# Strided queries, masked copies, ranks and a drain rearranged in an attention and mixture-of-experts kernel

## The chip, the cores and the metric

The kernel runs on one core of one Trainium2 chip. The metric is the time of one execution in device microseconds. The engines are called PE (matrix products), PEld (the loading of PE's weights), DVE (VectorE), ACT (ScalarE), POOL (GpSimd) and SP (SyncE, which here issues most of the plain loads).

## The reference

Eight batches with eight heads, 576 positions and 64 values a head. Heads 0 to 3 see a local window of 32 positions; heads 4 to 7 see every 32nd earlier position ("strided"). The 4608 rows of 512 values that come out go through a layer of eight experts, of which each row uses one:

```python
mask_local = (rel >= 0) & (rel < stride)
mask_strided = (rel >= 0) & (pos[None, :] % stride == pos[:, None] % stride)
attn = softmax(where(mask, q @ k.T / 8, -1e9)) @ v          # per head
x = attn.transpose(0, 2, 1, 3).reshape(B * S, H * D)        # 4608 x 512
logits = x @ w_gate + modality_bias[modality_id]            # 8 experts
e_idx = argmax(logits);  gate_w = softmax(logits)[e_idx]
out = gate_w * (relu(x @ w1[e_idx]) @ w2[e_idx])            # 512 -> 1024 -> 512
```

## The kernel before

**Attention** (the first 190 us or so). The batches are taken as four pairs (`bp` 0 to 3). Work comes in 32 units, alternately a `Local` (one local head of a batch pair) and a `Strided` (two strided heads of one batch). Iteration n of the main loop loads unit n+3, does the scores of unit n, the transposes (`turn`) of unit n-2 and the values of unit n-3, and prepares (`prep`) unit n+2. PE runs in exactly the order in which this code is written; the other engines are ordered by a scheduler, except where `pin` keeps instructions in the order of the code. Each engine takes its own instructions in its own order, and a tile's readers wait for its writers by semaphores.

`Local.prep` writes queries into a zeroed block tile `qd`, one half on DVE, one on ACT. `Strided.prep` makes the like tile `qz` from the loaded `qks`: POOL multiplies the queries, broadcast over two halves, by a 0/1 mask (L379; for unit 0 DVE does it). `Strided.scores` multiplies `qz` by the keys into `ss`, and DVE and ACT make the normalised exponentials `ens`. `Strided.turn` transposes these into `ts` in PSUM and copies them four times, each time with another 0/1 mask per partition, into `eb`: copies 0 and 2 on DVE (L424), 1 and 3 on ACT (L422). `Strided.values` multiplies `eb` by the values `vs` into `ot`.

**Routing** of a batch pair is a generator, `finish_pair` with `route` in it, of which the main loop takes POPS = 5 steps an iteration (the expert stage two steps an f-step). It transposes the rows, forms the logits `lg` and `lt`, and marks the chosen expert of each row in `oh` (`ohb` in bf16). The rank of a row within its expert needs a running count: DVE makes `cum` by nine dependent additions (L536) after a comparison, a reduction and an addition (L531 to L534). After RK = 14 further steps two matrix products give the ranks `rk` (L540, L541), DVE makes of them the list `posi`, and POOL scatters the pair's token rows from the tile `xt` to the DRAM buffer `xd`, by nine indirect DMAs (L557). `xt` has two buffers, so the first write of pair bp+2 to its `xt` (L352, in `Local.values`) waits for the scatter of pair bp. The row numbers `tok_sb`, loaded by SP, are copied into `xt` (L527).

**Experts.** 18 slots of 256 rows each of one expert (`ffn`), then one of 128 rows (`half_ffn`). A slot has eight f-steps of matrix products h (L832) and o (L846). POOL gathers the rows (`fx`, L701) and the weights (`raw`, L717) by indirect DMAs and sends the results out (L854; L776 for the half slot). ACT and DVE split the weights into two parts, `wh` and `wl`. Slots of pairs 1 and 2 are planned before the last pair is routed (`PHASES`).

Of the kernel before, what the change touches and what calls it, by code (L numbers as in the profile page):

```python
# [11 lines left out]
F32 = mybir.dt.float32  # L12
F32R = mybir.dt.float32r
BF16 = mybir.dt.bfloat16
# [6 lines left out]
P = 128  # L21
# [6 lines left out]
E = 8  # L28
# [10 lines left out]
LT, RK = 7, 14  # L39
# [10 lines left out]
C_HALF = C_P + 1  # L50
C_T = C_HALF + 2
# [22 lines left out]
def _constants():  # L74
    cf = np.zeros((P, C_N), np.float32)
    cf[:, C_ID:C_ID + P] = np.eye(P)
    cf[:, C_RE8:C_RE8 + E] = E - np.arange(E)
    cf[:, C_H:C_H + 2] = np.arange(P)[:, None] + P * np.arange(2)
    cf[:, C_SIO:C_SIO + 32] = np.arange(32)
    cf[:, C_P] = np.arange(P)  # L80
    cf[:, C_F:C_F + 4] = P * np.arange(4)
    cf[:64, C_HALF] = 1
    cf[64:, C_HALF + 1] = 1
# [90 lines left out]
def attention_moe(ctx: ExitStack, tc: tile.TileContext, a, out):  # L174
# [13 lines left out]
    warm = pa("warm")  # L188

# [71 lines left out]
    ets = zeros(2, [P, 4, 4, 2, 32], "et")  # L261
    for t in qds + ets:
        nc.vector.memset(t[:], 0.0)

# [92 lines left out]
    class Strided:  # L357
# [17 lines left out]
        def prep(self):  # L375
            self.qz = qz = lp.tile([P, 32, 2, 18], F32, tag="qz", name=f"qz{self.n}")
            q = self.qk[:, 0, :].rearrange("p (r q) -> p r q", q=18).unsqueeze(2).to_broadcast([P, 32, 2, 18])
            half = cf[:, C_HALF:C_HALF + 2].unsqueeze(1).unsqueeze(3).to_broadcast([P, 32, 2, 18])
            (nc.gpsimd if self.n else nc.vector).tensor_tensor(qz[:], q, half, ALU.mult)  # L379
# [31 lines left out]
        def turn(self):  # L411
# [4 lines left out]
            self.eb = eb = lp.tile([72, 4, 2, 2, 72], F32, tag="eb", name=f"eb{n}")  # L416
            src = tp[0:72].rearrange("p g (j x) -> p g j x", j=2)[:, :, :, 0:36].rearrange("p g j (h q) -> p g j h q", h=2)
            for t in range(4):
                dst = eb[:, :, :, :, 18 * t:18 * t + 18]
                on = cf[0:72, C_T + t:C_T + t + 1]  # L420
                if t % 2:
                    nc.scalar.activation(dst, src, AF.Copy, scale=on)  # L422
                else:
                    nc.vector.tensor_scalar(dst, src, on, None, ALU.mult)  # L424

        def values(self):
            n, eb, vs, b = self.n, self.eb, self.vs, self.b
            for g2 in range(2):
                ot = pa(f"ot{n}{g2}")[:, :288]
                for g in (2 * g2, 2 * g2 + 1):  # L430
                    for j in range(2):
                        c = (g % 2) * 144 + 72 * j
                        for h in range(2):
# [3 lines left out]
                                eb[:, g, j, h, :],  # L437
# [36 lines left out]
    def route(bp, xt, xcs):  # L474
# [45 lines left out]
        ohb = ap.tile([P, 9, E], BF16, tag="ohb", name=f"ohb{bp}")  # L520
        nc.vector.tensor_copy(ohb[:], oh[:])
# [8 lines left out]
        cum = ap.tile([P, 10, E], BF16, tag="cum", name=f"cum{bp}")  # L530
# [3 lines left out]
        nc.vector.tensor_scalar(cum[:, 0, :], low[:], float(T2 * bp // P), None, ALU.add)  # L534
        for i in range(9):
            nc.vector.tensor_tensor(cum[:, i + 1, :], cum[:, i, :], ohb[:, i, :], ALU.add)  # L536
# [3 lines left out]
        nc.tensor.matmul(rk, cb[:, M_TRI:M_TRI + P], ohb.rearrange("p t e -> p (t e)"), start=True, stop=False)  # L540
        nc.tensor.matmul(rk, cb[:, M_ONE:M_ONE + P], cum[:, 0:9, :].rearrange("p t e -> p (t e)"), start=False, stop=True)  # L541
        po = ap.tile([P, 9, E], F32, tag="po", name=f"po{bp}")
        nc.vector.tensor_tensor(po[:], rk.rearrange("p (t e) -> p t e", t=9), oh[:], ALU.mult)
# [4 lines left out]
        new = cum[:, 0, :]  # L548
        nc.vector.tensor_tensor(fst[:, bp, :], new, cnt[:, bp, :], ALU.subtract)
        if bp:  # L550
            nc.vector.tensor_tensor(stp[:, bp, :], fst[:, bp, :], fst[:, bp - 1, :], ALU.subtract)
        else:
            nc.vector.tensor_copy(stp[:, 0, :], new)
        nc.vector.tensor_tensor(cnt[:, bp + 1, :], cum[:, 9, :], fst[:, bp, :], ALU.subtract)
# [192 lines left out]
    def half_ffn(fp, le, xs):  # L747
# [10 lines left out]
        for f in range(8):  # L758
# [13 lines left out]
            settle(LAG)  # L772
        settle(0)
# [253 lines left out]
```

## Time and profile before

| what | us |
|---|---|
| median of the runs (3) | 624.02 |
| lowest and highest | 623.73, 792.28 |
| the profiled execution: time | 620.45 |
| the profiled execution: span of its trace | 618.6 |

The profiled execution's time is 1.85 us more than its span, and the median is 3.57 us more than the profiled execution. Times in the trace count from the span's start. In the timeline a row gives the start, the duration, the engine, the line, the operation and its tiles; the brackets give how long the engine had been idle ahead of it and what ended the wait. PEclk is the clock that PE was granted, as a share of full speed.

### The profile page before, as it was taken

How to read it: one execution, taken by the hardware profiler on the slowest of the kernel's cores; microseconds unless marked ns; L12 is line 12 of the kernel's file. 1: busy time of each engine (PE TensorE's matmuls, PEld its weight loads, DVE VectorE, ACT ScalarE, POOL GpSimd, SP SyncE). 2: the span in 40 equal slices, each digit the busy share in tenths (PEclk: the TensorE clock that was granted, in tenths of full speed). 3: DMA queues.
4: the chain of work that ended last, by engine and by line, in shares of the span. 5: the costliest groups of instructions: out<-in, count | busy, mean ns of one | idle time of the engine just before them, and what ended most of it. 6: DMA issues, size and time to landing. Idle time of an engine off the chain costs nothing.

```text
span 618.6 us, 15169 instructions
## 1 busy us (share of the span) xinstructions
PE 582.8 (94%) x5979; PEld 507.3 (82%) x5979; DVE 459.2 (74%) x1141; ACT 370.7 (60%) x755; POOL 254.9 (41%) x212
## 2 busy tenths in 40 slices
PE   7989898898989999899999999999999999999991
PEld 4767785686778988798998999998989999999990
DVE  7786886895979799697687777777777777777540
ACT  2657674675657666466665666665666665666540
POOL 1242154266173558854524444533533542432210
PEclk9999999797999999999999999999999999999996
DMA  8986787699365865674744854413422457342610
GB/s 291 296 268 193 210 274 281 181 310 369 107 233 100 251 208 158 166 268 104 204 173 103 205 184 77 104 33 74 103 52 54 105 155 220 85 67 72 231 42 20
DMA packets 66158, 102.50 MB, mean 166 GB/s; under 512 B 46815, under 2 KB 48095, under 8 KB 62496
## 3 DMA queue, kind: packets, MB, share of 16 engines
q0 software_dynamic: 19744, 58.57, 28.2%
q1 hardware_dynamic: 46048, 42.47, 27.5%
q8 instruction: 49, 0.80, 0.5%
q10 hardware_dynamic: 288, 0.41, 0.2%
q14 instruction: 29, 0.24, 0.1%
HBM read 123.66 MB, written 19.43 MB: 231 GB/s over the span
## 4 chain that ended last, share of the span: by engine, by line
PE 67%; DVE 12%; DMA 10%; ACT 3%; issue 3%; POOL 2%; ACTq 0%; POOLq 0%; DVEq 0%
PE h L832 31%; PE o L846 30%; DMA xd<-xt,posi 5%; DMA raw<-in_w,wi 2%; DMA vv<-in_vl 1%; DMA tok_sb<-in_tok 1%; DVE xt L352 1%; DMA cf_sb<-in_cf 1%; DVE ex L310 1%; ACT wh L867 1%; DVE mx L309 1%; DVE eb L424 1%; POOL xd L557 1%; PE o L334 1%; DVE wl L868 1%
## 5 line engine op out<-in xcount | busy, mean ns | idle before, releaser
L868 DVE TENSOR_TENSOR wl<-raw,wh 128x512 fp32r<-128x512 f32 x288 | 186.7, 687 | 78.2 <-ACT wh L867 77.8
L867 ACT CAST wh<-raw 128x512 fp32r<-128x512 f32 x288 | 164.0, 619 | 98.2 <-PE o L846 86.2
L832 PE MATMUL h<-xh,wh 128*128 128x256 f32 x576 | 163.4, 284 | 2.1 <-ACT wh L867 1.4
L832 PE MATMUL h<-xh,wl 128*128 128x256 f32 x576 | 163.1, 284 | 0.0
L832 PE MATMUL h<-xl,wh 128*128 128x256 f32 x576 | 162.0, 282 | 0.0
L717 POOL DMA_INDIRECT raw<-in_w,wi x72 | 84.9, 1179 | 174.4 <-DVE wl L868 159.7
L832 PEld LDWEIGHTS h<-xh,wh 128*128 128x128 f32 x576 | 108.7, 189 | 9.4 <-ACT wh L867 1.8
L846 PE MATMUL o<-wh,hh 128*128 128x512 f32 x288 | 114.7, 398 | 0.3 <-ACT hh L835 0.3
L832 PEld LDWEIGHTS h<-xl,wh 128*128 128x128 f32 x576 | 108.8, 189 | 6.3
L846 PE MATMUL o<-wl,hh 128*128 128x512 f32 x288 | 113.7, 395 | 0.0
L846 PE MATMUL o<-wh,hl 128*128 128x512 f32 x288 | 112.8, 394 | 0.0
L832 PEld LDWEIGHTS h<-xh,wl 128*128 128x128 f32 x576 | 108.3, 188 | 0.8
L835 ACT ACTIVATE hh<-h 128x256 fp32r<-128x256 f32 x144 | 55.3, 385 | 47.5 <-PE h L832 47.1
L837 DVE SCALAR_TENSOR_TENSOR hl<-h,hh 128x256 fp32r<-128x256 f32 x144 | 60.5, 420 | 11.7 <-ACT hh L835 11.6
L846 PEld LDWEIGHTS o<-wh,hl 128*128 128x128 f32 x288 | 53.8, 188 | 11.9
L379 POOL TENSOR_TENSOR qz<-qks,cf_sb 128x1152 f32<-128x1152 f32 x15 | 31.7, 2113 | 74.6 <-DMA qks<-in_qks 47.7
L846 PEld LDWEIGHTS o<-wh,hh 128*128 128x128 f32 x288 | 54.3, 188 | 7.9 <-ACT hh L835 0.5
L846 PEld LDWEIGHTS o<-wl,hh 128*128 128x128 f32 x288 | 54.3, 189 | 5.8
L701 POOL DMA_INDIRECT fx<-xd,li x36 | 47.2, 1312 | 21.3 <-issue 9.1
L854 POOL DMA_INDIRECT out<-y,le x36 | 44.3, 1229 | 21.7 <-ACT y L853 14.7
L557 POOL DMA_INDIRECT xd<-xt,posi x36 | 37.3, 1036 | 29.2 <-ACT xc L442 12.7
L311 ACT ACTIVATE ex<-ex 128x256 f32<-128x256 f32 (+1 forms) x32 | 14.0, 443 | 29.4 <-DVE ex L310 29.1
(181 smaller groups left out, 771.6 us busy)
## 6 DMA issues: line engine op xcount, KB each, us to landing
qk<-in_qkl SPq DMA_DIRECT2D x16, 592.0 KB
qks<-in_qks SPq DMA_DIRECT2D x16, 576.0 KB
vv<-in_vl SPq DMA_DIRECT2D x16, 520.0 KB
vs<-in_vs SPq DMA_DIRECT2D x16, 288.0 KB
raw<-in_w,wi POOLq DMA_INDIRECT x72, 3.4
vv<-in_vl SPq DMA_DIRECT2D x16, 65.0 KB
xd<-xt,posi POOLq DMA_INDIRECT x36, 5.9
fx<-xd,li POOLq DMA_INDIRECT x36, 5.5
```

What stands on the lines that cost most here:

```text
L311: nc.scalar.activation(ex[:, g0:g0 + gn, :], ex[:, g0:g0 + gn, :], AF.Exp, scale=0.125)
L379: (nc.gpsimd if self.n else nc.vector).tensor_tensor(qz[:], q, half, ALU.mult)
L557: lists.add(nc.gpsimd.indirect_dma_start(xd[0:(bp + 1) * T2, :], IOA(ap=posi[:, i:i + 1], axis=0), xt[:, i, :], None))
L701: nc.gpsimd.indirect_dma_start(xt[:, h, :], None, xd[0:xrows, :], IOA(ap=li[:, s, h:h + 1], axis=0))
L717: ins = nc.gpsimd.indirect_dma_start(raws[j].rearrange("p f c -> p (f c)"), None, a["w"], IOA(ap=wi[:, s, j:j + 1], axis=0), bounds_check= ...
L832: nc.tensor.matmul(hp, w[:, a1], x[:, c, :], start=(k == 0), stop=(k == 11))
L835: nc.scalar.activation(hh[:], hp, AF.Relu)
L837: nc.vector.scalar_tensor_tensor(hl[:], hp, 0.0, hh.bitcast(F32), ALU.max, ALU.subtract)
L846: nc.tensor.matmul(os[h], hx[:, m], w[:, 512:1024], start=(f == 0 and i == 0), stop=(f == 7 and i == 2))
L854: outs.add(nc.gpsimd.indirect_dma_start(out, IOA(ap=le[:, h, 0:1], axis=0), y[:], None, bounds_check=NT - 1, oob_is_err=False))
L867: nc.scalar.copy(wh[:, c], raw[:, c])
L868: nc.vector.tensor_tensor(wl[:, c], raw[:, c], wh[:, c].bitcast(F32), ALU.subtract)
```

## The change

There are five parts. (1) `qz` becomes two fixed tiles, zeroed once by POOL at the start, and each strided unit's queries are written by two half copies, one on DVE and one on ACT, pinned; POOL does none of it. (2) Of the four masked copies to `eb`, the two of DVE become one instruction with the mask as a broadcast operand; ACT keeps two; the layout of `eb` changes, so that the values' moving operand comes in four runs of 18. (3) The running count becomes one scan instruction over an (expert, tile) layout; the matrix of the rank product changes with it, and RK goes from 14 to 6. (4) An activation on a small tile at the start makes ACT load its table there. (5) A drain of POOL is put in f-step 0 of `half_ffn`. Constants that fall away, changes of line numbers and the `new` subtraction follow from these.

```diff
-LT, RK = 7, 14
+LT, RK = 7, 6
...
-    cb[:, M_TRI:M_TRI + P] = np.arange(P)[:, None] < np.arange(P)[None, :]
+    cb[:, M_TRI:M_TRI + P] = -(np.arange(P)[:, None] >= np.arange(P)[None, :]).astype(np.float32)
...
+    first = cp.tile([P, 1], F32, name="first")
+    nc.scalar.activation(first[:], idle[:, 0:1], AF.Exp)
...
+    qzs = zeros(2, [P, 32, 2, 18], "qz")
+    for t in qzs:
+        nc.gpsimd.memset(t[:], 0.0)
...
         def prep(self):
-            self.qz = qz = lp.tile([P, 32, 2, 18], F32, tag="qz", name=f"qz{self.n}")
...
-            (nc.gpsimd if self.n else nc.vector).tensor_tensor(qz[:], q, half, ALU.mult)
+            self.qz = qz = qzs[self.n % 2]
+            for h in range(2):
+                r = slice(64 * h, 64 * h + 64)
+                dst, src = qz[r, :, h, :], self.qk[r, 0, :].rearrange("p (r q) -> p r q", q=18)
+                pin(nc.scalar.copy(dst, src) if h else nc.vector.tensor_copy(dst, src))
...
-            for t in range(4):
-                dst = eb[:, :, :, :, 18 * t:18 * t + 18]
-                on = cf[0:72, C_T + t:C_T + t + 1]
-                if t % 2:
-                    nc.scalar.activation(dst, src, AF.Copy, scale=on)
-                else:
-                    nc.vector.tensor_scalar(dst, src, on, None, ALU.mult)
+            sh = [72, 8, 2, 36]
+            nc.vector.tensor_tensor(
+                eb[:, :, 0:2, :], src.unsqueeze(2).to_broadcast(sh),
+                cf[0:72, C_T:C_T + 2].unsqueeze(1).unsqueeze(3).to_broadcast(sh), ALU.mult)
+            for t in (2, 3):
+                nc.scalar.activation(eb[:, :, t, :], src, AF.Copy, scale=cf[0:72, C_T + t:C_T + t + 1])
...
-                                eb[:, g, j, h, :],
+                                eb[:, 2 * g + j, :, 18 * h:18 * h + 18],
...
-        nc.vector.tensor_tensor(sc[:], eb9(re8), nb(m8), ALU.is_lt)
-        low = ap.tile([P, E], F32, tag="low", name=f"low{bp}")
-        nc.vector.tensor_reduce(low[:], sc.rearrange("p t e -> p e t"), AX.X, ALU.add)
-        nc.vector.tensor_scalar(cum[:, 0, :], low[:], float(T2 * bp // P), None, ALU.add)
-        for i in range(9):
-            nc.vector.tensor_tensor(cum[:, i + 1, :], cum[:, i, :], ohb[:, i, :], ALU.add)
+        ohf, cuf = ohb.rearrange("p e t -> p (e t)"), cum.rearrange("p e t -> p (e t)")
+        nc.vector.tensor_tensor_scan(cuf, ohf, ohf, float(T2 * bp // P), ALU.add, ALU.bypass)
         for _ in range(RK):
             yield
...
             settle(LAG)
+            if f == 0:
+                pin(nc.gpsimd.drain())
```

**PE, the ranks of pair 0.** In the kernel before, this stands on PE right behind the strided scores that follow the routing products `lt` of pair 0 (the number behind a tile's name is only a count, and differs between the kernels):

```order
L202 MATMUL ts_1260<-cf_sb,ens_997 72x128 x4
L334 MATMUL o_1270<-vv_951,et_103 64x65 x8
L345 MATMUL o_1270<-vv_951,e_1134 32x65 x4
L334 MATMUL o_1287<-vv_951,et_103 64x65 x8
L298 LDWEIGHTS cb_sb
L298 MATMUL s_1308<-cb_sb 128x256
L302 MATMUL s_1308<-qk_949,qd_101 64x64 x8
```

and this, two iterations later, is where the ranks of pair 0 come:

```order
L202 MATMUL ts_1419<-cf_sb,ens_1258 72x128 x4
L334 MATMUL o_1429<-vv_1212,et_102 64x65 x8
L345 MATMUL o_1429<-vv_1212,e_1345 32x65 x4
L334 MATMUL o_1446<-vv_1212,et_102 64x65 x8
L540 LDWEIGHTS cb_sb
L540 MATMUL rk_1461<-ohb_1187,cb_sb 128x72
L541 LDWEIGHTS cb_sb
L541 MATMUL rk_1461<-cum_1196,cb_sb 128x72
L298 LDWEIGHTS cb_sb
L298 MATMUL s_1481<-cb_sb 128x256
```

Now the ranks come two iterations sooner, behind the first of these two groups of values:

```order
L201 MATMUL ts_1249<-cf_sb,ens_999 72x128 x4
L336 MATMUL o_1258<-vv_953,et_105 64x65 x8
L347 MATMUL o_1258<-vv_953,e_1135 32x65 x4
L336 MATMUL o_1275<-vv_953,et_105 64x65 x8
L538 LDWEIGHTS cb_sb
L538 MATMUL rk_1290<-ohb_1188,cb_sb 128x72
L539 LDWEIGHTS cb_sb
L539 MATMUL rk_1290<-cum_1197,cb_sb 128x72
L300 LDWEIGHTS cb_sb
L300 MATMUL s_1310<-cb_sb 128x256
```

So eight steps at five an iteration have moved the two products `rk` from behind the second next strided unit to ahead of the scores that come next, and the scatter on POOL, which follows from them, with it. The same move is made for pairs 1 and 2.

**DVE, one unit of each kind** (about 18 to 22 us in the profile before). Before, the twelve rows from the maximum of a strided unit's scores on:

```order
L400 TENSOR_REDUCE mxs_316<-ss_282 128x16
L424 TENSOR_SCALAR eb_332<-ts_327,cf_sb 72x16x18
L402 TENSOR_TENSOR exs_318<-ss_282,mxs_316 128x288
L350 TENSOR_SCALAR rs_350<-o_337 128x5
L351 RECIPROCAL rs_350<-rs_350 128x5
L424 TENSOR_SCALAR eb_332<-ts_327,cf_sb 72x16x18
L352 TENSOR_TENSOR xt_112<-o_337,rs_350 128x5x64
L405 TENSOR_REDUCE sms_321<-exs_318 128x16
L350 TENSOR_SCALAR rs_363<-o_354 128x4
L309 TENSOR_REDUCE mx_373<-s_375 128x4
L406 TENSOR_SCALAR sms_321<-sms_321 128x16
L351 RECIPROCAL rs_363<-rs_363 128x4
```

Now, the twelve rows from the same place on:

```order
L403 TENSOR_REDUCE mxs_322<-ss_288 128x16
L422 TENSOR_TENSOR eb_338<-ts_333,cf_sb 72x8x72
L405 TENSOR_TENSOR exs_324<-ss_288,mxs_322 128x288
L352 TENSOR_SCALAR rs_355<-o_342 128x5
L353 RECIPROCAL rs_355<-rs_355 128x5
L352 TENSOR_SCALAR rs_368<-o_359 128x4
L354 TENSOR_TENSOR xt_118<-o_342,rs_355 128x5x64
L353 RECIPROCAL rs_368<-rs_368 128x4
L311 TENSOR_REDUCE mx_378<-s_380 128x4
L354 TENSOR_TENSOR xt_118<-o_359,rs_368 128x4x64
L382 COPY qz_106<-qks_236 64x32x18
L408 TENSOR_REDUCE sms_327<-exs_324 128x16
```

The two `eb` instructions have become one, and a copy into `qz`, which waits for the load of `qks`, stands behind the last `xt` product and ahead of the sum of `exs` (the first of these copies, for the unit before, stood ahead of the piece). ACT's queue has the two `eb` copies together now, with its own half of `qz` behind them and the exponential of `exs` behind that.

**POOL, around the scatters of pairs 0 and 1.** Before:

```order
L379 TENSOR_TENSOR qz_1039<-qks_861,cf_sb 128x1152
L379 TENSOR_TENSOR qz_1300<-qks_1091,cf_sb 128x1152
L379 TENSOR_TENSOR qz_1459<-qks_1302,cf_sb 128x1152
L379 TENSOR_TENSOR qz_1637<-qks_1475,cf_sb 128x1152
L557 DMA xd<-xt_112,posi_1468 1152x528 x9
L379 TENSOR_TENSOR qz_1819<-qks_1641,cf_sb 128x1152
L526 MEMSET xt_122 128x9x14
L379 TENSOR_TENSOR qz_2080<-qks_1871,cf_sb 128x1152
```

Now, from the scatter of pair 0 to the first weight loads of the expert stage:

```order
L556 DMA xd<-xt_118,posi_1297 1152x528 x9
L528 MEMSET xt_128 128x9x14
L556 DMA xd<-xt_123,posi_2063 2304x528 x9
L716 DMA raw_2371<-in_w,wi_2292 128x2048
L716 DMA raw_2375<-in_w,wi_2292 128x2048
```

The products into `qz` are gone; between the scatters of pairs 0 and 1 only a small clearing of `xt` is left. Further on, the gathers `fx` stand more evenly between the loads `raw` than they did. The new drain stands on POOL behind the last `raw` load of the half slot and ahead of the last three sendings of results.

More of the change, by code (lines that the diff above doesn't have):

```diff
@@ L49 @@
 C_P = C_SIO + 32
-C_HALF = C_P + 1
-C_T = C_HALF + 2
+C_T = C_P + 1
 C_F = C_T + 4
@@ L519, in route @@
         nc.vector.tensor_tensor(oh[:], eb9(re8), nb(m8), ALU.is_equal)
-        ohb = ap.tile([P, 9, E], BF16, tag="ohb", name=f"ohb{bp}")
-        nc.vector.tensor_copy(ohb[:], oh[:])
+        ohb = ap.tile([P, E, 9], BF16, tag="ohb", name=f"ohb{bp}")
+        nc.vector.tensor_copy(ohb.rearrange("p e t -> p t e"), oh[:])
         nc.scalar.activation(lo[:], lo[:], AF.Exp)
@@ L528, in route @@
         nc.vector.reciprocal(xt[:, :, DM + 1], sm[:])
[L530 to L536 removed]
+        cum = ap.tile([P, E, 9], BF16, tag="cum", name=f"cum{bp}")
+        ohf, cuf = ohb.rearrange("p e t -> p (e t)"), cum.rearrange("p e t -> p (e t)")
+        nc.vector.tensor_tensor_scan(cuf, ohf, ohf, float(T2 * bp // P), ALU.add, ALU.bypass)
         for _ in range(RK):
@@ L539, in route @@
         rk = pa(f"rk{bp}")[:, 0:72]
-        nc.tensor.matmul(rk, cb[:, M_TRI:M_TRI + P], ohb.rearrange("p t e -> p (t e)"), start=True, stop=False)
-        nc.tensor.matmul(rk, cb[:, M_ONE:M_ONE + P], cum[:, 0:9, :].rearrange("p t e -> p (t e)"), start=False, stop=True)
+        nc.tensor.matmul(rk, cb[:, M_TRI:M_TRI + P], ohf, start=True, stop=False)
+        nc.tensor.matmul(rk, cb[:, M_ONE:M_ONE + P], cuf, start=False, stop=True)
         po = ap.tile([P, 9, E], F32, tag="po", name=f"po{bp}")
-        nc.vector.tensor_tensor(po[:], rk.rearrange("p (t e) -> p t e", t=9), oh[:], ALU.mult)
+        nc.vector.tensor_tensor(po[:], rk.rearrange("p (e t) -> p t e", t=9), oh[:], ALU.mult)
         pos = ap.tile([P, 9], F32, tag="pos", name=f"pos{bp}")
@@ L547, in route @@
         nc.vector.tensor_copy(posi[:], pos[:])
-        new = cum[:, 0, :]
-        nc.vector.tensor_tensor(fst[:, bp, :], new, cnt[:, bp, :], ALU.subtract)
+        new = ap.tile([P, E], BF16, tag="new", name=f"new{bp}")
+        nc.vector.tensor_tensor(new[:], cum[:, :, 0], ohb[:, :, 0], ALU.subtract)
+        nc.vector.tensor_tensor(fst[:, bp, :], new[:], cnt[:, bp, :], ALU.subtract)
         if bp:
@@ L552, in route @@
         else:
-            nc.vector.tensor_copy(stp[:, 0, :], new)
-        nc.vector.tensor_tensor(cnt[:, bp + 1, :], cum[:, 9, :], fst[:, bp, :], ALU.subtract)
+            nc.vector.tensor_copy(stp[:, 0, :], new[:])
+        nc.vector.tensor_tensor(cnt[:, bp + 1, :], cum[:, :, 8], fst[:, bp, :], ALU.subtract)
         for i in range(9):
```

8 lines of the change are left out of this document (2 added, 6 removed).

## The prediction

> **What bounds the kernel now.** I read the page first: busy shares, the slices' granted clock, and the chain that ended last.
>
> ```profile
> PE 582.8 (94%) x5979; PEld 507.3 (82%) x5979; DVE 459.2 (74%) x1141; ACT 370.7 (60%) x755; POOL 254.9 (41%) x212
> PEclk9999999797999999999999999999999999999996
> PE 67%; DVE 12%; DMA 10%; ACT 3%; issue 3%; POOL 2%; ACTq 0%; POOLq 0%; DVEq 0%
> ```
>
> PE is busy 94% and nothing in the change takes work off it, so there are only three kinds of time to win: gaps on PE, stretches in which PE ran at a lower clock (the slices with 7), and the ends of the span. The view by windows says where they lie (columns: window, its length, busy time of PE, PEld, DVE, ACT, POOL, then granted clock, DMA share, GB/s).
>
> ```profile
> 13.00:49.00 36.00, 32.09 (x721) 25.81 (x721) 28.50 (x83) 20.38 (x43) 11.02 (x9) 0.91 0.88 272
> 99.00:124.00 25.00, 20.36 (x410) 15.84 (x410) 18.20 (x66) 12.74 (x29) 5.73 (x4) 0.86 0.59 185
> 124.00:154.00 30.00, 27.49 (x551) 22.47 (x549) 22.27 (x90) 19.46 (x43) 19.88 (x19) 0.89 0.96 345
> 300.00:570.00 270.00, 270.00 (x1719) 244.38 (x1718) 202.41 (x370) 169.90 (x334) 109.48 (x93) 1.00 0.46 114
> ```
>
> In the middle of the expert stage PE has no gap and full clock: the change can do nothing there. Everything is in the attention stage and the tail. The timeline of PE gives the gaps (the rows with a bracket); the rows without one are there to price a slow stretch and a pair of units.
>
> ```profile
> 38.04 0.69 PE L302 MATMUL s<-qk,qd 128*64 128x64 f32 x16 [1.30 <-ACT ex L311]
> 44.62 1.04 PE L202 MATMUL ts<-cf_sb,ens 128*72 128x128 f32 x4 [1.17 <-DVE ens L409]
> 48.02 0.28 PE L298 MATMUL s<-cb_sb 128*128 128x256 bf16 x1
> 55.00 0.63 PE L202 MATMUL ts<-cf_sb,ens 128*72 128x128 f32 x4
> 57.04 0.77 PE L202 MATMUL xl<-cf_sb,xt 128*128 128x128 f32 x5
> 69.51 0.28 PE L298 MATMUL s<-cb_sb 128*128 128x256 bf16 x1
> 76.52 0.60 PE L202 MATMUL ts<-cf_sb,ens 128*72 128x128 f32 x4 [1.83 <-DVE cum L536]
> 78.73 0.27 PE L298 MATMUL s<-cb_sb 128*128 128x256 bf16 x1
> 103.17 0.77 PE L202 MATMUL t<-cf_sb,ex 128*128 128x128 f32 x5 [2.15 <-DVE xt L352]
> 116.16 0.42 PE L384 MATMUL ss<-cb_sb 128*128 128x288 bf16 x1 [1.18 <-DVE xt L352]
> 147.12 1.33 PE L202 MATMUL t<-cf_sb,ex 128*128 128x128 f32 x5 [2.49 <-DVE xt L352]
> 176.16 1.50 PE L480 MATMUL lg<-xc,wg_sb 128*32 128x256 f32 x24 [1.80 <-ACT xc L458]
> ```
>
> The transposes `ts` and the values behind them took 48.02 - 44.62 = 3.40 us after the gap at 44.62, and 57.04 - 55.00 = 2.04 undisturbed. At half the clock that stretch lost 1.36 us of a clock deficit of 1.7 (half of 3.40): 0.8 of the deficit. So the windows give the whole price: 13 to 49 us 0.09 x 36 x 0.8 = 2.6, 99 to 124 us 0.14 x 25 x 0.8 = 2.8, 124 to 154 us 0.11 x 30 x 0.8 = 2.6.
>
> **Part 1, POOL's products go.** The gaps come behind small DVE instructions that took far too long. Three of them, for two with what POOL did then, and one of the same kind when POOL was idle:
>
> ```profile
> 40.74 2.11 POOL L379 TENSOR_TENSOR qz<-qks,cf_sb 128x1152 f32<-128x1152 f32 x1 [1.39 <-DMA qks<-in_qks]
> 40.95 1.93 DVE L406 TENSOR_SCALAR sms<-sms 128x16 f32<-128x16 f32 x1
> 21.65 0.16 DVE L406 TENSOR_SCALAR sms<-sms 128x16 f32<-128x16 f32 x1
> 72.06 2.11 POOL L379 TENSOR_TENSOR qz<-qks,cf_sb 128x1152 f32<-128x1152 f32 x1 [9.71 <-PE t L202]
> 72.54 1.65 DVE L553 COPY stp<-cum 128x8 bf16<-128x8 bf16 x1
> 113.09 1.66 DVE L534 TENSOR_SCALAR cum<-low 128x8 bf16<-128x8 f32 x1
> ```
>
> Sixteen elements take 0.16 us, and 1.93 us beside POOL's product: DVE's instruction ends when POOL's does. This holds DVE for about 1.5 to 1.9 us in each disturbed pair of units, and PE shows it as 1.17 us at 44.6, 1.83 us at 76.5 and 1.18 us at 116.2. Without POOL's products these gaps go: **1.17** with half of the first window's clock loss, **1.3**; **1.83**, which no slow stretch follows; **1.18** with the **2.8** of 99 to 124 us, whose slow slices follow that gap.
>
> What takes their place is on DVE and ACT.
>
> ```profile
> L424 DVE TENSOR_SCALAR eb<-ts,cf_sb 72x288 f32<-72x288 f32 x32 | 16.0, 501 | 2.4 <-PE ts L202 1.0 <-ACT eb L422 0.7
> L290 ACT COPY qd<-qk 64x576 f32<-64x576 f32 x16 | 10.7, 668 | 0.4
> L434 PE MATMUL ot<-eb,vs 72*64 72x72 f32 x512 | 20.5, 236 | 0.5 <-ACT eb L422 0.3
> L310 DVE TENSOR_TENSOR ex<-s,mx 128x320 f32<-128x320 f32 x16 | 7.5, 471 | 0.2
> L310 DVE TENSOR_TENSOR ex<-s,mx 128x256 f32<-128x256 f32 x16 | 6.5, 406 | 0.1
> 17.16 0.44 DVE L290 COPY qd<-qk 64x576 f32<-64x576 f32 x1
> ```
>
> The half copies have the shape of the `qd` copies: 0.44 us on DVE, 0.67 on ACT. The merged `eb` copy reads PSUM and has 576 elements; two PSUM rows (256 in 406 ns, 320 in 471 ns) give 1.02 ns an element and so about 0.73 us, against 2 x 0.50 before. DVE per strided unit: -1.00 + 0.73 + 0.44 = +0.17 us; ACT: +0.67 us, 16 times. A pair of units took 9.22 us on PE from 69.51 to 78.73, 7.4 without the gap of 1.83 in it; DVE is busy 74% and ACT 60% over the span, so neither becomes the bound by its sum; by order they can, since DVE's `qz` copy now waits for the load of `qks` itself, with the sum of `exs`, `ens` and then PE's `ts` behind it. I charge **-0.7** in all for small waits of this kind, a quarter of 16 x 0.17 = 2.7, with 0 and -2.7 as bounds. POOL's two clearings of the fixed tiles come before anything that PE waits for, and cost nothing. The values' products take 20.5 us in all; that their moving operand now has runs of 18 has no row here, and I take 0 for it, the half copies' runs of 18 and 32 being the nearest thing, with a tenth, 2 us, either way as bounds.
>
> Of the first 34 us little can be had. DVE waits there for the row numbers, and loads fill the queues (DMA share 0.88 in that window):
>
> ```profile
> 34.23 2.09 DVE L527 COPY xt<-tok_sb 128x9 int32<-128x9 int32 x1 [2.76 <-DMA tok_sb<-in_tok]
> ```
>
> Whatever PE wins ahead of this (by an earlier table load, part 4, or a DVE copy that no longer lies beside POOL) is waited off here; what stays is the copy itself, 2.09 us beside another product of POOL, under which the 1.30 at 38.04 lies. I take **0.8** for parts 1 and 4 up to 40 us, between 0 and 4.
>
> **Part 3, the ranks.** This is the largest term. DVE waits for the scatter of the pair before last, because `xt` has two buffers:
>
> ```profile
> 84.62 1.15 POOL L557 DMA_INDIRECT xd<-xt,posi  x1 [2.54 <-DVE qd L290]
> 95.03 0.96 POOL L557 DMA_INDIRECT xd<-xt,posi  x1 [0.30 <-ACT exs L403]
> 102.62 0.82 DVE L352 TENSOR_TENSOR xt<-o,rs 128x320 f32<-128x320 f32 x2 [4.16 <-DMA xd<-xt,posi]
> 146.58 0.82 DVE L352 TENSOR_TENSOR xt<-o,rs 128x320 f32<-128x320 f32 x2 [3.73 <-DMA xd<-xt,posi]
> ```
>
> The scatter follows the ranks, which come two iterations, one pair of units, sooner: 7.4 us undisturbed. The waits are 4.16 and 3.73, so they go, and with them PE's gaps of **2.15** and **2.49** and the slow stretch behind the last, **2.6**: 7.2 us. What is late next is a smaller thing: PE now reaches the product `rk` before DVE has made its input.
>
> ```profile
> 69.77 0.18 DVE L521 CAST ohb<-oh 128x72 bf16<-128x72 f32 x1
> ```
>
> Pair 0's `ohb` was made from 69.77 on; PE, which had pair 0's `rk` just ahead of 78.73, would now be at it at 69.51; and the scan stands four rows behind `ohb`, at some 0.15 to 0.2 us each, so ready at about 70.6. So PE waits about 1.1 us for each of three pairs, **-3.3**. The scan has no row in this trace; nine additions of 0.15 us hold DVE for 1.4 and a 72-element row for 0.2, so the wait is between 0.3 and 2 a pair, -1 to -6 for the three.
>
> **Rest of the attention stage and the start of the experts.** The gap of 1.80 at 176.16 waits on ACT, which gets more work but is released sooner; I count **1.0** of it, from 0 to 1.8.
>
> **Part 5, the drain.** The last rows of the span are these.
>
> ```profile
> L1023 POOLq DRAIN  x3: 40/107/6598, 611.1 to 618.3; - x3
> 594.22 1.03 POOL L854 DMA_INDIRECT out<-y,le  x1 [10.12 <-ACT y L853]
> ```
>
> One drain at the end of POOL's queue takes 6.6 us, the other two 0.1 or less. If it works off what POOL has gathered in the whole kernel, the one put in `half_ffn` does most of that in POOL's idle 10.12 us ahead of the last sendings, where it is hidden with 3.5 us to spare; I take **6.0**, between 0 (each drain costs the same) and 6.6.
>
> **The sum**: 1.17 + 1.3 + 1.83 + 1.18 + 2.8 - 0.7 + 0.8 + 7.2 - 3.3 + 1.0 + 6.0 = 19.3 us. From 620.45 this gives 601.15 in the conditions of the profiled execution; the median of the runs stood 3.57 us above it, so 604.7.
>
> [...] The slices with a 7 (108 to 124 and 139 to 155 us) are those that hold the gaps at 116.16 and 147.12, while those at 76.52 and 103.17 lie in slices with 9, and the stretch of 3.40 us follows a gap of only 1.17. [...]
>
> **Rivals.** [...] (b) *The last drain stays long*: its 6.6 us are the price of any drain behind DMAs. For: one row at the end is all that shows it. Against: two drains of the same group took 0.1. It loses 6.0: 610.7. (c) *The scatters slow down*: DVE's copies now run beside POOL's DMA issues, and if they stop these as POOL's product stopped DVE, each of nine issues goes from 0.96 us to 2.1 or more, the scatter ends 10 us later, and the 7.2 come back: 611.9. Against: the first and the last issue of pair 0 took 1.15 and 0.96 us, and DVE's `qd` copies, which have the same shape, lay among them. (d) *Slower*: DVE, in order, stands behind the landing of `qks`.
>
> ```profile
> 43.36 0.35 DVE L352 TENSOR_TENSOR xt<-o,rs 128x256 f32<-128x256 f32 x1
> ```
>
> One landed at 40.74 (POOL's row), and DVE reached the place of the copy, behind this `xt`, 2.97 us later. If loads land 5 us later against the work, since the work is now faster and the loads are not, each of the 13 strided units from there loses 2.0 us, and 0.4 for each of the slow microseconds that such gaps bring, one a unit: 13 x 2.4 = 31, so 636, slower than before. It decides from a delay of 3 us on. (e) *Nothing happens* but for the ends: 620 or more, when DVE's slow instructions have another cause.
>
> [...]
>
> **How the numbers follow.** The forecast 0.54; (b) 0.18; (a) 0.10; (c) 0.05; the terms of small waits all at their worse bounds (ranks -6, small waits -2.7, no 1.0: 610.4) 0.06; (d) 0.04; (e) 0.03. A measurement of this kernel can tell about 2%, 12.5 us: faster is under 611.5. The forecast and, of (a), (b), (c) and the small waits, about six in ten lie below: 0.54 + 0.23 less a little for the forecast's own upper edge, 0.75. Slower (above 636.5) 0.04, for (d) and worse; the same 0.21. The range: down, the better bounds of the start (3.2 more), the gap at 176 (0.8), the drain (0.6), the ranks (2.3), the small waits (0.7) and the values (2.0) would come to 9.6, of which 8.7 gives 596; up, it takes in (a), (b), (c) and the small waits with 1 us over, 613.
>
> **What will show it.** No POOL row of `qz`, and DVE's small instructions at 0.16 throughout; the `xt` waits for `xd` gone from the chain of waits; clock 1.00 in all windows from 49 us on; two or three new PE gaps of 0.3 to 2 us that end at `rk`; a drain at about 585 us and a last one far under 6.6 us. Wrong would be: PE gaps that end at `qz` or at `ens` behind a wait for `qks`, clock 0.9 in spite of closed gaps, issues of `xd` of 2 us.

## The result, and the profile after

The changed kernel took 605.13 us, the median of four runs (602.7 to 608.89), against 623.88 for the kernel before; the ratio, taken over the runs and not from the medians, is 0.9721, with a 95% interval of 0.9645 to 0.9797. The forecast was 604.7. One run of the kernel before, 792.28 us, is left out of the ratio. The profiled execution took 602.70 us, 17.75 less than that of before, where the sum of the forecast had 19.3.

The page of the changed kernel, the lines that were shown of before:

```profile
PE 578.0 (96%) x5979; PEld 505.6 (84%) x5979; DVE 442.4 (74%) x1100; ACT 381.6 (64%) x772; POOL 221.8 (37%) x199
PEclk9879998999999999999999999999999999999999
PE 81%; DMA 6%; DVE 4%; issue 3%; ACT 3%; POOL 2%; SPq 0%; POOLq 0%; DVEq 0%; ACTq 0%
```

DVE's share of the chain that ended last fell from 12% to 4%, and the two late slices with a 7 in PEclk are gone. But there is an 8 and a 7 now in the second and third slice, and an 8 in the seventh. The view by windows (the columns as in the prediction) says the same:

```profile
13.00:49.00 36.00, 30.32 (x685) 24.50 (x684) 24.38 (x76) 21.66 (x46) 2.42 (x3) 0.86 0.87 260
49.00:99.00 50.00, 47.28 (x1035) 38.57 (x1036) 36.02 (x122) 37.60 (x81) 9.20 (x10) 0.97 0.82 269
99.00:124.00 25.00, 24.08 (x577) 19.81 (x571) 19.47 (x78) 19.01 (x41) 7.97 (x8) 1.00 0.73 242
124.00:154.00 30.00, 26.19 (x536) 20.97 (x537) 21.06 (x99) 20.31 (x44) 7.40 (x9) 1.00 0.87 310
```

From 99 to 154 us the clock is full, as forecast. From 13 to 49 us it went the other way, 0.91 to 0.86, and PE is busy 30.32 us where it was 32.09. From 49 to 99 us the prediction had a clock of 1.00 as a sign of being right; it is 0.97, where the kernel before had 1.00. The timeline of PE has the gaps behind that:

```profile
15.07 2.11 PE L391 MATMUL ss<-qks,qz 128*36 128x18 f32 x64 [1.79 <-ACT e L327]
35.99 1.04 PE L201 MATMUL ts<-cf_sb,ens 128*72 128x128 f32 x4 [3.89 <-DVE ens L412]
69.72 0.21 PE L538 MATMUL rk<-ohb,cb_sb 128*128 128x72 bf16 x1 [0.79 <-DVE rs L352]
93.09 0.68 PE L201 MATMUL ts<-cf_sb,ens 128*72 128x128 f32 x4 [1.66 <-DVE ens L412]
109.71 0.20 PE L538 MATMUL rk<-ohb,cb_sb 128*128 128x72 bf16 x1 [0.79 <-DVE rs L352]
127.68 0.39 PE L304 MATMUL s<-qk,qd 128*64 128x64 f32 x5 [1.45 <-issue]
133.38 0.63 PE L201 MATMUL ts<-cf_sb,ens 128*72 128x128 f32 x4 [0.54 <-DVE ens L412]
```

Two waits for `rk` are where the forecast put them. The gaps at 35.99 and 93.09 were not foreseen. DVE's timeline names their cause: one instruction, the copy of the row numbers into `xt`, which stands in DVE's queue ahead of `ens`.

```profile
33.19 0.25 DVE L529 COPY xt<-tok_sb 128x9 int32<-128x9 int32 x2 [3.09 <-DMA tok_sb<-in_tok]
34.05 0.94 DVE L292 COPY qd<-qk 64x576 f32<-64x576 f32 x1
34.92 0.93 DVE L412 TENSOR_TENSOR ens<-exs,sms 128x288 f32<-128x288 f32 x1
92.50 0.18 DVE L529 COPY xt<-tok_sb 128x9 int32<-128x9 int32 x1 [3.19 <-DMA xd<-xt,posi]
```

At 33 us it waits for the load of the row numbers, at 92 for the scatter that frees the buffer of `xt`. (The two instructions of 0.9 us behind the first wait lie beside POOL's remaining products for `bias`, from 34.01 on.) How long the first wait is differs from run to run with the landing of this load, as the experiments show.

The table follows the program by the start of the strided scores (`ss`) on PE, for every third strided unit, counted from 0, in the profiled executions. The difference is the sum up to each place; the last column has the terms that the forecast adds between the row above and this one.

| strided unit | before | after | difference | the forecast's terms |
|---|---|---|---|---|
| 6 | 66.02 | 65.38 | -0.64 | 1.17 + 1.3 + 0.8 = 3.3 |
| 9 | 90.99 | 89.91 | -1.08 | 1.83 - 1.1 = 0.7 |
| 12 | 126.28 | 120.92 | -5.36 | 2.15 + 1.18 + 2.8 - 1.1 = 5.0 |
| 15 | 160.12 | 154.25 | -5.87 | 2.49 + 2.6 - 1.1 = 4.0 |
| `yh`, behind PE's last product | 604.86 | 594.57 | -10.29 | 1.0 |
| end of the span | 618.6 | 600.9 | -17.7 | 6.0 |

(The -0.7 for small waits has no place of its own.) So the total is right by errors that cancel: the first 66 us gave 0.64 of 3.3 and units 12 to 15 gave 0.51 of 4.0, while the stretch behind unit 15 gave 4.42 where 1.0 stood, and the end 7.4 for 6.0.

The drains of the changed kernel: the one in the half block, and those at the end.

```profile
L773 POOLq DRAIN  x1: 8952/8952/8952, 572.6 to 572.6; - x1
L1024 POOLq DRAIN  x3: 46/107/299, 599.3 to 600.6; - x3
583.93 1.03 POOL L855 DMA_INDIRECT out<-y,le  x1 [10.12 <-ACT y L854]
```

The new drain takes 8.95 us, from 572.6 to 581.6 (until 573.81 POOL still has the issue of a weight load in hand), and is hidden: POOL's idle time ahead of the next sending is 10.12 us as before. The last drain fell from 6.6 to 0.3 us.

### The profile page after: what moved, and what is told of

Its sections match the earlier page's. It is cut to its first block, busy times and chain, and to the rows that moved or that the text cites. A ratio compares the mean times of both kernels' runs of the same rounds, so it can differ in the third digit from the quotient of the medians.

```text
span 600.9 us, 15171 instructions
## 1 busy us (share of the span) xinstructions
PE 578.0 (96%) x5979; PEld 505.6 (84%) x5979; DVE 442.4 (74%) x1100; ACT 381.6 (64%) x772; POOL 221.8 (37%) x199
## 4 chain that ended last, share of the span: by engine, by line
PE 81%; DMA 6%; DVE 4%; issue 3%; ACT 3%; POOL 2%; SPq 0%; POOLq 0%; DVEq 0%; ACTq 0%
PE h L833 34%; PE o L847 33%; DMA xd<-xt,posi 4%; PE s L304 2%; PE o L336 2%; POOL xd L556 2%; PE lg L482 1%; PE xs L201 1%; DMA tok_sb<-in_tok 1%; PE xl L201 1%; DMA qks<-in_qks 1%; PE ss L391 1%; PE ot L436 1%; PE ts L201 1%; PE t L201 1%
## 5 line engine op out<-in xcount | busy, mean ns | idle before, releaser
L716 POOL DMA_INDIRECT raw<-in_w,wi x72 | 89.3, 1241 | 187.8 <-DVE wl L869 165.8
L700 POOL DMA_INDIRECT fx<-xd,li x36 | 39.6, 1101 | 13.4 <-issue 10.6
L325 ACT COPY et<-t 64x512 f32<-64x512 f32 x32 | 18.5, 579 | 19.2 <-PE t L201 18.8
L815 DVE COPY xs<-cols 128x1024 uint16<-128x1024 uint16 x34 | 24.4, 773 | 7.7 <-DMA cols<-rows 7.7
```

What stands on the lines that cost most here:

```text
L700: nc.gpsimd.indirect_dma_start(xt[:, h, :], None, xd[0:xrows, :], IOA(ap=li[:, s, h:h + 1], axis=0))
L716: ins = nc.gpsimd.indirect_dma_start(raws[j].rearrange("p f c -> p (f c)"), None, a["w"], IOA(ap=wi[:, s, j:j + 1], axis=0), bounds_check= ...
L815: pin(nc.vector.tensor_copy(dst, cols[:, :, w].rearrange("p h c q -> p c h q")))
```

## The experiments

They ran in three groups, each on a chip of its own, with the kernel before timed beside each group: 653.79, 653.36 and 616.63 us. Times are therefore compared within a group, or as ratios to the kernel before with their intervals. That the first two groups stand 30 us higher than the first comparison is taken up first.

### The changed kernel on another chip, and what starves there

> The changed kernel again, as the yardstick for the runs beside it. Both theories: 603 to 609 us, PE's gaps at the same places as in its first profile (about 3.9 us ahead of ts near 36 us, 1.7 ahead of ts near 93 us).

It took 652.85 us, a ratio of 0.9966 (0.9932 to 0.9999): nearly nothing of the gain is left. In the window 76 to 86 us, in which POOL issues the scatter of pair 0 in both profiles, the first row is that of this run, the second that of the first profile of the changed kernel:

```profile
76.00:86.00 10.00, 4.62 (x42) 3.35 (x38) 0.46 (x1) 0.85 (x2) 7.56 (x8) 0.53 0.60 232
```

```profile
76.00:86.00 10.00, 9.86 (x246) 7.95 (x243) 8.43 (x27) 8.34 (x18) 7.28 (x8) 1.00 0.98 355
```

PE ran 42 products instead of 246, DVE one instruction instead of 27; POOL did its part at the same pace. PE's timeline in this run shows a few products, then nothing for half a microsecond to one, with "issue" as the cause, that is, no cause that the profile sees:

```profile
80.17 0.50 PE L336 MATMUL o<-vv,et 128*64 128x65 f32 x5 [0.94 <-issue]
81.62 0.27 PE L336 MATMUL o<-vv,et 128*64 128x65 f32 x1 [0.95 <-issue]
83.05 0.44 PE L347 MATMUL o<-vv,e 64*32 64x65 f32 x4 [0.81 <-issue]
```

I call this starving for instructions; it is a name for what is seen, since the rows do not show what the engines lacked. Over the whole span PE's waits of this kind come to 29.1 us here and 3.0 in the first profile of the changed kernel. They are not the whole price, since the products between them come slowly too: from strided unit 7 to unit 8, around this scatter, it takes 94.23 - 74.02 = 20.2 us, and 80.88 - 73.73 = 7.2 in the first profile.

> The kernel before, with a trace from the same chip as the runs beside it. The last drain 6.6 us and DVE's instructions of 1.6 us and more beside POOL's products in both theories. On the chip of the four runs before this one, engines starved for instructions (issue) while POOL issued the scatters: if that is a matter of the chip, the starved stretches of about 12 us stand in this kernel as well, at its later scatters; if the change brought them, they do not.

The kernel before on the second chip: 653.72 us, 0.9983 (0.9932 to 1.0033). Its profiled execution was 16 us above its median, so it is used only for where things lie. It starves too, in the scatter of pair 0, later in the program:

```profile
84.00:94.00 10.00, 4.78 (x50) 2.93 (x47) 1.33 (x3) 1.40 (x4) 7.56 (x9) 0.71 0.82 283
```

So the starving is not the change's doing. That the change alters which work the scatters fall on is read from the order of the program; the run with 14 steps, below, bears on what that costs.

### Ranks: later, alone, and with the row numbers moved

> The changed kernel with 14 steps ahead of the ranks instead of 6. Theory 1 (the sooner ranks are worth the scatter waits, less the three waits for the scan): the scatter of pair 0 ends some 7 us later, DVE's wait for it grows from 3.2 to 8 us or more, and the time is 5 to 9 us more, 610 to 614; PE's waits of 0.79 us ahead of the ranks are gone. Theory 2 (with POOL's products gone the scatter would be early enough anyway): within 2 us of the changed kernel.

```diff
-LT, RK = 7, 6
+LT, RK = 7, 14
```

It took 640.71 us, 0.9802 (0.9746 to 0.9857), 12 us less than the changed kernel beside it: both theories fell, which had expected more time or the same. Two things differ in the profiles. The first lies ahead of anything that the edit moves: up to 70 us DVE's order is the same in both, with the row-number copy in the same place, but the load of the row numbers, which SP issued at 27.96 and 27.71 us, landed sooner. This run's row comes first, that of the changed kernel beside it second:

```profile
31.72 0.25 DVE L529 COPY xt<-tok_sb 128x9 int32<-128x9 int32 x2 [0.36 <-DMA tok_sb<-in_tok]
33.56 0.25 DVE L529 COPY xt<-tok_sb 128x9 int32<-128x9 int32 x2 [3.25 <-DMA tok_sb<-in_tok]
```

PE's gap near 35 us is 1.22 us, not 3.51, and unit 4 begins at 40.19 instead of 44.60. That part is chance, as far as the record shows, and whether the other three runs had it is not known. The second follows from the edit: from unit 15 to `yh` it takes 633.64 - 175.47 = 458.2 us, where the changed kernel takes 645.60 - 179.56 = 466.0. The window of the fourth scatter, of the changed kernel and then of this one:

```profile
235.00:262.00 27.00, 21.87 (x129) 17.93 (x128) 13.04 (x35) 9.18 (x18) 19.22 (x18) 0.98 0.92 283
```

```profile
238.00:265.00 27.00, 27.00 (x175) 24.33 (x174) 23.53 (x71) 15.82 (x31) 17.20 (x16) 1.00 0.76 233
```

With 6 steps POOL issues 18 DMAs there without a pause, the nine of the scatter first, and PE starves in the second half of them; with 14 steps the scatter is split in three and six, with pauses of 2 to 3 us between, and PE does not wait at all. So in these two profiles, on a chip where engines starve, the sooner ranks cost 7.9 us behind unit 15.

> The kernel before with part 3 alone: the scan and 6 steps ahead of the ranks. Theory 1 where engines do not starve: 4 to 6 us less than the kernel before, by the scatter waits and the slow stretch behind them less the waits for the scan. Theory 1 where they starve: the third scatter moves into the dense part of attention, and the kernel is 8 to 14 us slower than the kernel before. Theory 2 (the place of the scatter costs nothing): 4 to 6 us less in either case.

This is the kernel before with the scan, the other matrix and `RK = 6`, and nothing else. It ran in the third group, on a chip where nothing starves (PE's waits on "issue" 5.7 us in all): 613.13 us against 616.63, 0.9913 (0.9867 to 0.9958). Theory 1 had 4 to 6 us less; the medians give 3.5, the ratio 5.4 with an interval from 2.6 to 8.2. Theory 2 had the same for such a chip. So the run does not part the two, since nothing starved. What it shows beside the number is where part 3 pays. From unit 15 to `yh` it takes 598.30 - 157.85 = 440.5 us. The changed kernel takes 440.3 (594.57 - 154.25), and the kernel before took 444.7 (604.86 - 160.12, in its first profile). The gap of 1.80 ahead of `lg` is not there: the logits of the last pair run in another place, between the first products of the expert stage. Nor are two later gaps that the kernel before has, and that the prediction does not name:

```profile
186.44 0.39 PE L832 MATMUL h<-xh,wh 128*128 128x256 f32 x1 [0.74 <-ACT ls L488]
259.37 0.39 PE L832 MATMUL h<-xh,wh 128*128 128x256 f32 x1 [1.41 <-ACT wh L867]
```

Together these three are 1.80 + 0.74 + 1.41 = 3.95 us, most of the 444.7 - 440.5 = 4.2 by which the two differ. The rows of this run are:

```profile
72.12 0.21 PE L536 MATMUL rk<-ohb,cb_sb 128*128 128x72 bf16 x1 [0.54 <-DVE rs L350]
169.85 0.39 PE L829 MATMUL h<-xh,wh 128*128 128x256 f32 x1 [0.21 <-ACT wh L864]
170.84 1.49 PE L480 MATMUL lg<-xc,wg_sb 128*32 128x256 f32 x20
```

> The changed kernel as the yardstick of this group. Where engines do not starve for instructions during the scatters: 603 to 609 us; where they do: 650 to 655.

603.7 us, 0.9763 (0.9712 to 0.9814): where nothing starves, the first result comes again.

> The changed kernel with the copy of the row numbers on POOL and 14 steps ahead of the ranks, so that the third pair's scatter falls behind the densest part of attention again. Theory 1 (while POOL issues a scatter the other engines get few instructions, so a scatter costs most where PE's instructions are shortest): 12 to 17 us less than the changed kernel where engines starve, 636 to 641; where they do not, the scatter waits come back on xt and it is 0 to 5 us slower than with the copy on POOL alone. Theory 2 (the gain of the run with 14 steps came from the order of DVE around the row numbers, which moved with it): 5 us less than the changed kernel in either case.

```diff
-        nc.vector.tensor_copy(xt[:, :, DM].bitcast(I32), tok[:, 9 * bp:9 * bp + 9])
+        nc.gpsimd.tensor_copy(xt[:, :, DM].bitcast(I32), tok[:, 9 * bp:9 * bp + 9])
...
-LT, RK = 7, 6
+LT, RK = 7, 14
```

600.21 us, 0.972 (0.9675 to 0.9766): 3.5 less than the changed kernel beside it, though the intervals overlap. It does not decide between the theories: nothing starved, and the kernel with the copy on POOL alone, which theory 1 compares with, was not run on this chip. Two effects of opposite sign stand in its profile. The gap near 35 us is 0.92 and the `ts` behind it take 0.60 us, where the changed kernel beside it has 1.04 behind a gap of 2.85, so that unit 4 begins at 39.20 instead of 44.93; and the three gaps behind unit 15 are back, as in the kernel before:

```profile
33.24 0.60 PE L201 MATMUL ts<-cf_sb,ens 128*72 128x128 f32 x4 [0.92 <-DVE ens L412]
166.66 1.50 PE L482 MATMUL lg<-xc,wg_sb 128*32 128x256 f32 x24 [1.78 <-ACT xc L460]
176.60 0.39 PE L833 MATMUL h<-xh,wh 128*128 128x256 f32 x1 [0.62 <-ACT ls L490]
249.17 0.39 PE L833 MATMUL h<-xh,wh 128*128 128x256 f32 x1 [0.79 <-ACT wh L868]
```

From unit 15 on it takes 594.63 - 149.55 = 445.1 us, 4.8 more than the changed kernel there (597.38 - 157.06 = 440.3). So in part 3 the 8 steps are worth 4 to 5 us behind unit 15. What they are worth ahead of it this run cannot say, since the copy moved with them.

> The same with 11 steps ahead of the ranks, one iteration sooner than with 14 and one later than with 6. Theory 1: the third pair's scatter lies between the two places, so the time lies between those of the two (where engines starve 640 to 647), unless the scatter meets a dense unit. Theory 2: 5 us less than the changed kernel, as with 14 steps.

The same with `RK = 11`: 605.14 us, 0.9769 (0.9698 to 0.984). Its four runs are 600.49, 601.91, 608.38 and 609.87, and one profile cannot say what parts them. Its profile has unit 15 at 148.11 and `yh` at 593.47, 445.4 us again: 11 steps do not bring the gain behind unit 15 that 6 bring. For the starving this run says nothing.

### The row numbers on POOL

> The copy of the row numbers into xt is on POOL instead of DVE. Theory 1 (DVE, in order, stands at this copy and holds back the queue behind it): the waits of 3.1 us at 30 to 33 us, 3.2 at 89 to 92 and 1.8 at 131 to 133 leave DVE, PE's gaps of 3.89, 1.66 and 0.54 close and so do the slow stretches behind the first two (some 2 and 1.5 us): 5 to 9 us less than the changed kernel, 596 to 600. Theory 2 (the loads bind the first 50 us and the scatter binds xt itself): other waits, for qks, qk or vv and for xd, take the place: less than 2 us of difference.

This is the first change of the diff above alone: the copy goes to POOL, and the steps stay at 6. It took 647.69 us, 0.9918 (0.9886 to 0.995), 5.2 less than the changed kernel beside it. The two intervals overlap a little (0.9932 to 0.9999 there); the profile decides. Unit 4 begins at 39.67 instead of 44.60, and the lead stays: unit 9 98.66 for 102.85, unit 15 174.38 for 179.56. The gap ahead of `ts` is closed. In this run's DVE timeline the one wait over 0.2 us between the scores and `ens` is 0.70 us for a small load:

```profile
31.33 0.18 DVE L222 CAST modf<-modi 128x36 f32<-128x36 int32 x1 [0.70 <-DMA modi<-in_mod]
32.01 0.44 DVE L412 TENSOR_TENSOR ens<-exs,sms 128x288 f32<-128x288 f32 x1
```

Theory 1 is borne out at its lower edge. POOL's copy waited for the row numbers until 33.25 us, and PE did not: in the first 40 us it was the place of the copy in DVE's queue that held PE. Theory 1's later waits at the copy do not stand in the changed kernel of this group either, so for them the run shows nothing.

### The queries back on POOL

> The changed kernel with the strided queries multiplied by the mask on POOL again. Theory 1 (POOL's products hold DVE's instructions for 1.5 to 1.9 us each, and these were worth what the sum of the prediction gave): DVE instructions of 1.6 us and more beside each product, 5 to 8 us more than the changed kernel, 610 to 614. Theory 2 (most of that was waited off at the row numbers in the first 66 us; only the later ones count): 2 to 3 us more, 607.

```diff
-            for h in range(2):
-                r = slice(64 * h, 64 * h + 64)
-                dst, src = qz[r, :, h, :], self.qk[r, 0, :].rearrange("p (r q) -> p r q", q=18)
-                pin(nc.scalar.copy(dst, src) if h else nc.vector.tensor_copy(dst, src))
+            (nc.gpsimd if self.n else nc.vector).tensor_tensor(qz[:], q, half, ALU.mult)
```

(`q` and `half` as before, into the two fixed tiles, which need no clearing then.) 650.25 us, 0.995 (0.9919 to 0.9981): 2.6 less than the changed kernel beside it, and the two intervals overlap. Both theories expected more time. The slow DVE instructions are back as expected, which shows that POOL's products are their cause:

```profile
32.06 2.10 DVE L529 COPY xt<-tok_sb 128x9 int32<-128x9 int32 x2 [2.94 <-DMA tok_sb<-in_tok]
50.28 2.39 DVE L412 TENSOR_TENSOR ens<-exs,sms 128x288 f32<-128x288 f32 x1
70.41 1.74 DVE L548 TENSOR_TENSOR fst<-new,cnt 128x8 bf16<-128x8 bf16 x1
```

and PE's gap ahead of `ts` is 3.41 us with 3.51 in the changed kernel. So in the order that DVE has with the rest of the change, POOL's products cost no time that can be measured here. On a chip where nothing starves this was not tried.

### The drain left out, and put elsewhere

> The changed kernel without the drain in the half block. Theory 1 (that drain works off in POOL's idle time what the last drain would work off behind the end): the last drain 6 to 6.6 us, and 6 to 7.4 us more from PE's end to the end of the span than with it (6.3 us there), the rest unchanged. Theory 2 (the end is shorter for another reason, POOL's fewer instructions among them): less than 1 us more.

660.08 us, 1.0111 (1.0016 to 1.0206). The nearest kernel of its group with the drain in the half block, the one without the early table load, took 652.53. From `yh` to the end of the span it is 657.5 - 643.95 = 13.6 us against 647.0 - 640.58 = 6.4 there: 7.1 us more at the end. The last drain:

```profile
L1022 POOLq DRAIN  x3: 40/107/6598, 650.1 to 657.2; - x3
```

is 6598 ns, to the nanosecond that of the kernel before. Theory 1 holds.

> The changed kernel with its extra drain in the tenth expert slot instead of the half block. Theory 1 (a drain takes time in proportion to the indirect DMAs since the drain before): about 3 us of last drain, and some 3 us for the one in the middle, hidden by POOL's waits for weights there. Rival 1 (any one early drain makes the last one short): 0.3 us. Rival 2 (the last drain pays only for the DMAs just before it): 6 us or more.

```diff
-            if f == 0:
-                pin(nc.gpsimd.drain())
...
+                if k == 9 and f == 7:
+                    pin(nc.gpsimd.drain())
```

658.47 us, 1.0084 (1.0049 to 1.0119), 1.6 less than without any. The drain in the slot and the last one:

```profile
L976 POOLq DRAIN  x1: 3653/3653/3653, 439.7 to 439.7; - x1
L1024 POOLq DRAIN  x3: 46/107/5117, 649.1 to 654.8; - x3
```

Of the 186 indirect DMAs, 124 lie ahead of the first and 62 behind it, so proportion would give 4.4 and 2.2 us of the 6.6; it is 3.65 and 5.12. The 3.65 begin with the issue of a weight load that POOL had in hand until 441.44; from there on the drain lasts 1.9 us, and 1.9 + 5.1 = 7.0 is near the 6.6 of a single drain. So neither proportion nor a price of the last few DMAs alone: the last drain took 6.60 us with no drain among the 186 DMAs and 5.12 with 62 of them behind the earlier drain. What it waits for stays open. For the change only the other end matters: with three DMAs behind the drain in the half block, the last one takes 0.3 us.

### The early table load left out

> The changed kernel without the early activation, so that ACT loads its table ahead of the first copy into qd, as before. Theory 1 (what is won ahead of 33 us is waited off at the row numbers): 0.7 to 1.3 us later at the first scores, within 0.5 us from 37 us on, and no difference in the time. Theory 2 (the early load is worth its 1.28 us): 1 to 1.3 us later throughout.

652.53 us, 1.0 (0.9966 to 1.0034), against 0.9966 (0.9932 to 0.9999) with it in the first group: no difference that can be told. The load is late again and is not seen at the end:

```profile
5.91 1.28 ACT L290 ACT_TABLE_LOAD   x1 [5.91 <-DMA qk<-in_qkl]
```

The first strided scores begin at 9.52 us, and at 8.06 and 8.20 in the two other variants of this group; but unit 4 begins at 40.84 instead of 44.58 and 42.94, since PE's gap ahead of `ts` is 1.20 us (5.05 and 3.00 there) and the `ts` behind it take 0.60 us (1.04 there). DVE waited for the row numbers until 32.34 here, and until 34.36 and 32.40 there. So what is won ahead of 33 us is waited off at this copy, and how much is lost there differs with the landing of the load and with the slow stretch, which stands behind the two longer gaps and not behind that of 1.20.

## Why the prediction was right or wrong

**The total** is right, 605.13 for 604.7, and that is partly luck. The sum behind it is not right term by term, as the table shows. It came to 19.3 us where the profiles differ by 17.75, and the median stood 2.43 us above the profiled execution where the forecast had 3.57, which took back most of the rest. On the one chip with starving engines where both kernels were timed, the medians are 0.9 us apart: there the forecast would have been far off.

**Part 5** (6.0): right in that the drain in the half block shortens the last one, shown by leaving it out (6.60 us again, 0.30 with it). The size was 7.1 to 7.4, because the last drain fell by all but 0.3 and the short instruction ahead of it became shorter too (in the profiles 1790 ns before, 248 after). Rival (b) fell.

**Part 1** (1.17 + 1.3, and 0.8 for the start): the step that failed is "Without POOL's products these gaps go". The long DVE instructions went, so rival (e) fell, and with them the gap of 1.17; a gap of 3.89 came ahead of it, with a slow stretch behind (clock 0.50 from 35.99 to 40 us). The prediction had read the wait for the row numbers, and wrote that what PE wins ahead of it is waited off; it did not follow the copy's place in DVE's queue, ahead of `ens`. Moving that copy gave 5.2 us in the one group, and with 14 steps beside it unit 4 began 5.7 us sooner in another. The run with POOL's products put back says that they cost no measurable time in this order, on a chip that starves. The costs of what was added were right:

```profile
L436 PE MATMUL ot<-eb,vs 72*64 72x72 f32 x512 | 19.5, 229 | 0.0
L422 DVE TENSOR_TENSOR eb<-ts,cf_sb 72x576 f32<-72x576 f32 x16 | 12.0, 751 | 2.5 <-PE ts L201 1.3 <-DMA vs<-in_vs 0.5
L382 ACT COPY qz<-qks 64x576 f32<-64x576 f32 x16 | 10.8, 673 | 1.3 <-DMA qks<-in_qks 1.0
L382 DVE COPY qz<-qks 64x576 f32<-64x576 f32 x16 | 7.2, 448 | 1.2 <-DMA qks<-in_qks 1.2
L534 DVE TENSOR_TENSOR_SCAN cum<-ohb 128x72 bf16<-128x72 bf16 x4 | 1.2, 306 | 0.0
```

0.75 us for the merged `eb` (0.73 forecast), 0.45 and 0.67 for the halves of `qz` (0.44 and 0.67), and the values' products at 229 ns for 236, so their runs of 18 cost nothing. DVE and ACT waited 2.2 us in all for `qks` at these copies, so rival (d) fell.

**Part 3** (2.15 + 2.49 + 2.6 - 3.3): "The waits are 4.16 and 3.73, so they go" failed for the first, which went over to the row-number copy, 3.19 us, with 1.66 on PE. Behind unit 12 the gap of 2.49 and its slow stretch did go, but new gaps (1.45, 0.54, and four under 1) took most of it back; most of these have no releaser in the profile. The waits for `rk` were 0.79, not 1.1, though the scan takes 306 ns, not 200; two of the three show in the first profile, all three in that of the same kernel on the starving chip. Alone, the part measures 3.5 to 5.4 us, and its trace has some 4 of them behind unit 15: there the term "1.0 of it" was too small. It was put down to ACT and not to part 3, which moves the logits of the last pair, and the gaps of 0.74 and 1.41 in the expert stage were put at nothing: the prediction took its view of that stage from 300 us on. Why the wait for `wh` at 259 us goes with the sooner ranks is not shown.

**The clock** (1.3 + 2.8 + 2.6): the late stretches went with their gaps, as forecast, and not as in the prediction's (a), to which it gave 0.10: that they stay and the three terms are not won. New ones came with the gaps at 15, 36 and 93 us. Behind the gap of 1.79 at 15.07 the granted clock was 0.50 (64 products in 2.11 us), behind that of 3.89 at 35.99 it was 0.50 up to 40 us, and behind that of 1.66 at 93.09 it was 0.59 up to 95.5. After a gap of 1.57 in the run on the third chip the same 64 took 1.30, as they do at 1.00 in the first profile (at 23.61 us). The length of the gap alone does not decide: in the kernel before, the clock was 0.52 behind the gap of 1.17 at 44.62 us, and 1.00 behind that of 1.83 at 76.52. What decides is not shown.

**Rival (c)**, POOL's issues slowed by DVE's copies, fell: the issues of `xd` keep a mean of 1.02 us (1.04 before), and the seven of them that lay beside one of DVE's copies took 0.96 to 1.31. What two of the chips had is the reverse, a scatter beside which the other engines starve, and no rival had that.

## What to carry to other kernels

When a wait is removed, follow the queue of the engine that waited to the next instruction that can block, and look at what stands behind it: here a copy of nine elements a partition, which needed a load, took back most of what was forecast for the first 66 us: 0.64 us of 3.3 were left. A kernel's last drain may be worth more than a stage's tuning; here one drain in POOL's idle time near the end took 7 us off. And time a change on more than one chip: the same two kernels were 2 to 3% apart in two comparisons and 0 to 0.7% apart on another chip.

## What was not expected of the hardware

On two of the chips PE, DVE and ACT ran few instructions while POOL issued indirect scatters: 42 products in 10 us instead of 246, 25 to 32 us of "issue" waits on PE in the span where the other traces have 3 to 6. Whether this belongs to the chip or to what else ran on it then was not settled. On the first of these chips the scatter of pair 0, nine issues in a row beside short products, cost the changed kernel some 13 us (20.2 for 7.2 from unit 7 to unit 8); with the fourth scatter split by pauses of 2 to 3 us PE did not wait at all.

The last drain of POOL is long, 6.60 us, unless another stands ahead of it: it takes 5.12 behind one in the tenth slot and 0.30 behind one in the half block. Those drains last 1.9 and 7.7 us from the end of the issue in hand, behind 124 and 183 of the 186 indirect DMAs, and the last one loses 1.48 and 6.30 us by them: neither is in proportion to the DMAs ahead.
